# Sparse attention and a rational feed-forward layer: residue-split scores, batched normalisation, a chunk pipeline and a computed order of instructions

## The chip, the cores and the metric

The kernel runs on 1 core of one Trainium2 chip. The metric is device time in microseconds (us). Engines are named as the profile does: PE (TensorE, with PEld for its weight loads), DVE (VectorE), ACT (ScalarE), POOL (GpSimd), SP (SyncE, which here only issues transfers). A "q" behind an engine's name in a profile line ("SPq") means the engine's sequencer issuing a transfer.

## The reference

```
q, k, v: [8 batches, 8 heads, 576 tokens, 64], f32
scores = q @ k^T / 8
heads 0..3: keep 0 <= i-j < 32                      (local)
heads 4..7: keep j <= i and i % 32 == j % 32        (strided)
attn = softmax(scores);  o = attn @ v
x = o as [4608, 512];  h = x @ w_in                 (512 x 2048)
P = a0 + a1 h + a2 h^2 + a3 h^3
Q = 1 + |b0| |h| + |b1| h^2
out = (P / (Q + 1e-6)) @ w_out                      (2048 x 512, f32 out)
```

## The kernel before

The kernel takes 9 chunks of 512 tokens one after another: attention of one batch, first product, rational function, second product. Three parts matter here. Attention treats each head and each key tile by itself: scores into one bank, a mask added by a matmul with the identity, an exponential on ACT, a matmul with the values (with a column of ones, so that the row sums come along), then a reciprocal and a multiplication per head.

```python
ev_rc = emit(QDVE, Sdve, lambda d, ...: d.reciprocal(
    rcol[rl][r0:r0 + ns, 0:1], acc[r0:r0 + ns, VST * j + 64:VST * j + 65]), ...)
ev_nm = emit(QDVE, Sdve, lambda d, ...: d.tensor_scalar(
    XR[xslot][r0:r0 + ns, h * D:(h + 1) * D], acc[r0:r0 + ns, VST * j:VST * j + 64],
    rcol[rl][r0:r0 + ns, 0:1], None, op0=Alu.mult), ...)
```

The dense part has one set of buffers, and the output tile is copied by DVE:

```python
for f in range(NF):                     # 16 tiles of the first product, two banks
    psh = ps_h[f % 2]
    ... 4 matmuls (Win x XT) ...
    ACT: hbT[:, f, :] = copy(psh)
... rational function on hbT in pieces of 128 x 2048, one z and one u buffer ...
for m in range(TPC):                    # second product, one bank
    ... 16 matmuls (LG x Wout) ...
    DVE: outsb = copy(ps_out)
    POOL: store outsb
```

The casts from f32 to bf16 are issued by POOL, batch by batch, two heads at a time; the order in which instructions stand on each engine is written by hand.

The softmax here doesn't subtract the row's maximum and nothing guards it: scores larger than these inputs give would overflow.

## Time and profile before

| | before |
|---|---|
| median (range) | 924.05 us (923.52 to 924.86), 3 runs |
| busy, share of the span | PE 64%, DVE 50%, ACT 37% |
| mean granted clock (see the caution under "Reading the second hundred") | 0.724 |
| period per chunk, read from the timeline | about 99 us |

These lines are from the page of the kernel before. First the busy times; then rows of 40 slices of 23.1 us each, one digit a slice (busy share in tenths, for PEclk the granted clock in tenths); then the chain of waits that ended last, as shares of the span; then groups of instructions (count, busy us, mean ns of one, idle time before them and what ended it).

```profile
PE 593.8 (64%) x2704; PEld 255.2 (28%) x2704; DVE 460.7 (50%) x1001; ACT 345.3 (37%) x569; POOL 154.4 (17%) x167
...
PE   0493496469744985499628974698549854915706
...
DVE  0131059522954098416941495319540984393681
ACT  0131155406460437124531555053704371261540
...
PEclk9999975589556955596559755795569555967959
...
PE 53%; DVE 23%; ACT 15%; SPq 3%; DMA 2%; issue 2%; POOL 2%; DVEq 0%; POOLq 0%
...
L626 PE MATMUL ps_out<-Wout,lgt 128*128 128x512 bf16 x576 | 148.2, 416 | 152.0 <-DVE lgt L594 130.8
...
L516 ACT ACTIVATE hbt<-ps_h 128x512 bf16<-128x512 f32 x144 | 86.0, 597 | 309.4 <-PE ps_h L507 309.4
L435 DVE RECIPROCAL rcol<-ps_acc 128x1 f32<-128x1 f32 (+1 forms) x320 | 51.1, 160 | 268.5 <-PE ps_acc L407 266.8
...
L443 DVE TENSOR_SCALAR X<-ps_acc,rcol 128x64 bf16<-128x64 f32 (+1 forms) x320 | 90.8, 284 | 11.4
...
L304 POOL DMA_DIRECT2D ks<-in_k_dram x32 | 80.5, 4383 | 4.0 <-issue 4.0
```

No engine is full. The digits of PE and DVE go up and down in turn: the stages stand one behind the other, and the chain is handed from PE to DVE to ACT. The clock row sits at 5 to 7 for most of each period. Normalising costs DVE 51.1 + 90.8 = 142 us, in 640 small instructions.

### The profile page before, as it was taken

What the parts mean: (1) busy time and instruction counts of PE and PEld (TensorE: products, weight loads), DVE (VectorE), ACT (ScalarE), POOL (GpSimd) and SP (SyncE); (2) the same over time, 40 slices, a digit from 0 to 9 for tenths busy, and PEclk for the clock granted to TensorE, in tenths of its full rate; (3) what the DMA queues carried; (4) which work ended last, traced back from release to release, by engine and by line L of the source; (5) the groups of instructions that cost most, each with busy time, mean ns of one, the idle gap of its engine ahead of it and who ended that gap; (6) DMA issues with size and microseconds to landing.
All of it is one profiled execution on the core that took longest, in us unless ns stands there. A gap on an engine that the chain in (4) does not pass through costs nothing.

```text
span 924.9 us, 7533 instructions
## 1 busy us (share of the span) xinstructions
PE 593.8 (64%) x2704; PEld 255.2 (28%) x2704; DVE 460.7 (50%) x1001; ACT 345.3 (37%) x569; POOL 154.4 (17%) x167
## 2 busy tenths in 40 slices
PE   0493496469744985499628974698549854915706
PEld 0241142224321342134213432244213421302202
DVE  0131059522954098416941495319540984393681
ACT  0131155406460437124531555053704371261540
POOL 9986000240006000600020000000000000000000
PEclk9999975589556955596559755795569555967959
DMA  9999901490109010931051010101010000100001
GB/s 120 137 156 192 99 19 20 36 116 25 26 8 128 24 26 13 94 71 26 14 49 59 13 26 16 50 24 25 0 46 23 1 1 18 57 0 23 23 0 45
DMA packets 180868, 42.73 MB, mean 46 GB/s; under 512 B 175712, under 2 KB 178016, under 8 KB 180832
## 3 DMA queue, kind: packets, MB, share of 16 engines
q0 software_dynamic: 118016, 27.80, 30.7%
q1 hardware_dynamic: 62816, 14.47, 9.4%
q8 instruction: 21, 0.34, 0.2%
q14 instruction: 15, 0.12, 0.0%
HBM read 36.98 MB, written 18.87 MB: 60 GB/s over the span
## 4 chain that ended last, share of the span: by engine, by line
PE 53%; DVE 23%; ACT 15%; SPq 3%; DMA 2%; issue 2%; POOL 2%; DVEq 0%; POOLq 0%
PE ps_out L626 16%; PE ps_h L507 14%; PE ps_score L371 8%; PE ps_score L384 8%; PE ps_acc L407 7%; ACT lgt L573 7%; ACT qmt L581 5%; DVE lgt L594 5%; DVE chz L589 3%; DVE X L443 3%; ACT ET L391 3%; DVE outsb L636 2%; SPq L481 2%; DVE qmt L543 1%; DVE chu L554 1%
## 5 line engine op out<-in xcount | busy, mean ns | idle before, releaser
L626 PE MATMUL ps_out<-Wout,lgt 128*128 128x512 bf16 x576 | 148.2, 416 | 152.0 <-DVE lgt L594 130.8
L391 ACT ACTIVATE ET<-ps_score 128x192 bf16<-128x192 f32 (+5 forms) x352 | 126.6, 369 | 225.0 <-PE ps_score L384 195.5
L516 ACT ACTIVATE hbt<-ps_h 128x512 bf16<-128x512 f32 x144 | 86.0, 597 | 309.4 <-PE ps_h L507 309.4
L435 DVE RECIPROCAL rcol<-ps_acc 128x1 f32<-128x1 f32 (+1 forms) x320 | 51.1, 160 | 268.5 <-PE ps_acc L407 266.8
L407 PE MATMUL ps_acc<-vb,ET 128*128 128x65 bf16 (+3 forms) x784 | 127.0, 244 | 79.0 <-ACT ET L391 76.2
L371 PE MATMUL ps_score<-qT,kT 64*128 64x192 bf16 (+5 forms) x352 | 129.2, 367 | 28.7 <-DMA kT<-ks 28.7
L626 PEld LDWEIGHTS ps_out<-Wout,lgt 128*128 128x128 bf16 x576 | 57.8, 106 | 239.9 <-DVE lgt L594 132.7
L407 PEld LDWEIGHTS ps_acc<-vb,ET 128*128 128x128 bf16 (+3 forms) x784 | 75.7, 118 | 136.1 <-ACT ET L391 99.0
L636 DVE COPY outsb<-ps_out 128x512 f32<-128x512 f32 x36 | 24.9, 692 | 151.6 <-PE ps_out L626 151.6
L645 POOL DMA_DIRECT2D out_dram<-outsb x36 | 19.7, 548 | 468.3 <-DVE outsb L636 468.3
L443 DVE TENSOR_SCALAR X<-ps_acc,rcol 128x64 bf16<-128x64 f32 (+1 forms) x320 | 90.8, 284 | 11.4
L289 POOL DMA_DIRECT2D vb<-in_v_dram x40 | 36.3, 939 | 289.2 <-PE ps_acc L407 289.2
L304 POOL DMA_DIRECT2D ks<-in_k_dram x32 | 80.5, 4383 | 4.0 <-issue 4.0
L384 PE MATMUL ps_score<-MS,IDN 128*128 128x512 bf16 (+2 forms) x192 | 78.1, 407 | 0.9
L304 POOL DMA_DIRECT2D qs<-in_q_dram x32 | 77.0, 3952 | 3.4 <-issue 3.4
L573 ACT ACTIVATE lgt<-qmt,consts 128x2048 bf16<-128x2048 bf16 x36 | 69.4, 1990 | 15.9 <-DVE qmt L543 15.9
L507 PE MATMUL ps_h<-XT_0,Win 128*128 128x512 bf16 x144 | 55.3, 384 | 28.9 <-DMA XT_3<-X 28.9
L581 ACT ACTIVATE qmt<-lgt 128x2048 bf16<-128x2048 bf16 x36 | 65.6, 1896 | 0.0
L507 PE MATMUL ps_h<-XT_1,Win 128*128 128x512 bf16 x144 | 55.3, 384 | 0.0
L507 PE MATMUL ps_h<-XT_2,Win 128*128 128x512 bf16 x144 | 55.3, 384 | 0.0
L507 PE MATMUL ps_h<-XT_3,Win 128*128 128x512 bf16 x144 | 55.3, 384 | 0.0
L371 PEld LDWEIGHTS ps_score<-qT,kT 64*128 64x128 bf16 (+1 forms) x352 | 36.5, 104 | 65.6 <-DMA kT<-ks 28.8
(27 smaller groups left out, 496.6 us busy)
## 6 DMA issues: line engine op xcount, KB each, us to landing
out_dram<-outsb POOLq DMA_DIRECT2D x36, 256.0 KB, 2.3
qs<-in_q_dram POOLq DMA_DIRECT2D x32, 144.0 KB, 9.2
ks<-in_k_dram POOLq DMA_DIRECT2D x32, 144.0 KB, 9.5
vb<-in_v_dram POOLq DMA_DIRECT2D x32, 128.0 KB, 4.7
Win<-in_moe_w_in_dram POOLq DMA_DIRECT2D x4, 512.0 KB, 16.5
Wout<-in_moe_w_out_dram POOLq DMA_DIRECT2D x16, 128.0 KB, 22.0
XT_0<-X SPq DMA_TRANSPOSE x36, 3.1
XT_1<-X SPq DMA_TRANSPOSE x36, 2.4
```

The costliest lines, as they stand in the source:

```text
L304: lambda p, b=b, pair=pair, src_t=src_t, dst_t=dst_t: p.dma_start(dst_t[b, pair, :, :].rearrange("s (hh d) -> s hh d", hh=2), src_t[b, 2 * ...
L371: e.matmul(ps[0:nk, 0:x1 - x0], kT[tslot][pbase:pbase + 64, tk0:tk0 + nk], qT[tslot][pbase:pbase + 64, x0:x1], start=True, stop=False),
L384: e.matmul(ps[0:nk, 0:W], IDN[0:nk, 0:nk], mrhs, start=False, stop=True),
L391: a.activation(ET[esl][0:nk, 0:W], ps[0:nk, 0:W], AF.Exp, scale=0.125),
L407: return e.matmul(acc[rb:rb + M, VST * j:VST * j + 65], ET[esl][0:nk, ov0 - x0:ov0 - x0 + M], vb[slot][0:nk, ktile, h, 0:65], start=False, ...
L435: d.reciprocal(rcol[rl][r0:r0 + ns, 0:1], acc[r0:r0 + ns, VST * j + 64:VST * j + 65]),
L443: d.tensor_scalar(XR[xslot][r0:r0 + ns, h * D:(h + 1) * D], acc[r0:r0 + ns, VST * j:VST * j + 64], rcol[rl][r0:r0 + ns, 0:1], None, op0=Al ...
L507: e.matmul(psh[:, 0:CH], Win[kk][:, f * 128:(f + 1) * 128], XT[cs][kk][:, 0:CH], start=(kk == 0), stop=(kk == NK1 - 1)),
L516: a.activation(hbT[:, f, :], psh[:, 0:CH], AF.Copy),
L573: lambda a, qmT=qmT, lgT=lgT, f0=f0: a.activation(lgT[:, f0:f0 + G, :], qmT[:, f0:f0 + G, :], AF.Ln, bias=eps1_ap, scale=1.0),
L581: lambda a, qmT=qmT, lgT=lgT, f0=f0: a.activation(qmT[:, f0:f0 + G, :], lgT[:, f0:f0 + G, :], AF.Exp, scale=-1.0),
L626: e.matmul(pso[:, 0:Fout], LG[0][:, kk, m * 128:(m + 1) * 128], Wout[kk][:, 0:Fout], start=(kk == 0), stop=(kk == NK2 - 1)),
```

## The change

Its intent: compute the strided heads as dense small problems (tokens are split by their residue modulo 4, so that the mask wastes less), join exponentials into wide calls, normalise a whole tile of 128 tokens and 8 heads with two DVE instructions, double the buffers of the dense part, move the output copies to ACT, and let a list scheduler (an estimate of each instruction's cost, a priority key, and the rule "the free engine takes the ready instruction with the smallest key") compute the order in which the instructions stand on each engine. The diff rewrites nearly the whole kernel; its core:

```diff
-  NQT = 6; qT, kT [128, NKT*128] per head pair      # one bank, 352 score calls
-  ev_rc = reciprocal(... one head ...)               # x320
-  ev_nm = tensor_scalar(... one head ...)            # x320
+  o2 = add("DVE", lambda d: d.reciprocal(rc[:, :, :], psA[:, :, 64:65]), ..., 0.25, key - 20)
+  o3 = add("DVE", lambda d: d.tensor_tensor(x.rearrange("x (h d) -> x h d", h=8),
+           psA[:, :, 0:64], rc.to_broadcast([128, 8, 64]), op=Alu.mult), ..., 0.75, key - 20)
-  z, u, hbT, qmT, lgT, t3T: one buffer each, pieces of 128 x 2048
+  NHB = 2; NT3 = 2; NU = 2; NGB = 4                  # pieces of 128 x 4096
-  DVE tensor_copy(outsb, ps_out)
+  ACT activation(OS, psO, Copy)
-  casts issued per batch and head pair, by hand-written order
+  for b in range(B):                                 # all 24 casts, with no dependence at all
+      for nm, s_, d_ in (("q", q, qc), ("k", k, kc), ("v", v, vc)):
+          add("POOL", lambda e: e.dma_start(d_[b]..., s_[b]...), [], 1.2, key, g, 5.0)
+  ... relayouts ql<-qc, kl<-kc and transposes, all on SP, each with an assumed cost of 0.1 us ...
+  add("SP", fn, [cast[nm, b].ops], 0.1, key, grel, 3.0)
+  pr.schedule()                                      # list scheduler: order for each engine
   ... (cut)
```

The names in the new kernel: `qc`, `kc`, `vc` are the bf16 copies in device memory, `ql`, `kl` a second layout of them, `qS`, `kS`, `qL`, `kL` the transposed tiles for strided and local heads; `psS` holds scores, `psA` attention outputs, `XR` the normalised tile, `XT` its transpose, `psH` and `psO` the two products, `ZZ`, `UU`, `T`, `GB` the rational function.

## The prediction

> **What bounds it now.** Nothing is saturated: the page gives PE 64% of the span, DVE 50%, ACT 37%, and the chain of waits is handed around (PE 53%, DVE 23%, ACT 15%). The kernel runs its stages one after another. The timeline shows a period of about 99 us per chunk: some 65 us of attention mixed with the rational chain, then 14.4 us of second product (16 matmuls in 3.64 us, four times, evacuations of 0.70 us between them) and 13.8 us of first product (64 matmuls, 216 ns apart), during which DVE and ACT nearly stand still (ACT waits 309 us for the first product's banks). The granted clock alternates: 0.5 for about 65 us, 1.0 for about 34 us. [...]attention, with its small waits, runs at 0.5 throughout.
>
> **Work after the change (all estimates from trace durations).**
> - DVE. Rational chain in 8x512 pieces: the 2048-wide operations take 0.69 to 0.81 us (scalar, uncontended) and 1.23 us (two tensors); doubled width adds about 0.53 and 1.07, so about 15.7 us a group, 18 groups, 282 us (was about 302, with contention). Normalising: 40 x (0.17 + about 0.7) = 35 us instead of 51 + 91 = 142. The 25 us of output copies go to ACT. Sum about 325 us with gaps, instead of 461. POOL now issues about 150 small output transfers; where POOL issued transfers, a scalar operation took 1.35 instead of 0.75 us, so I add 30 us: about 355.
> - ACT. First-product copies 86, Ln/Exp 135, output copies 22, exponentials 45 (was 127: about 40,000 columns in 48 wide calls): about 290 us.
> - PE. Products 1152 x 0.22 = 253 us at full clock. Attention per batch: 80 score matmuls, 132 value matmuls, many of odd shapes. In the trace a 256-column matmul that alternates between 64 and 128 rows takes 0.21 to 0.22 us at full clock, about twice its streaming time. [...]The new order still alternates shapes, so I take 18 to 24 us a batch, 150 to 190 in all. Sum 400 to 440 us at full clock.
> - SP queue: about 25 plain issues (0.43), 8 transposes (1.25) and 5 X transposes (1.25 to 4) a batch, 27 to 41 us: close, not the limit.
>
> **Critical path.** Start: casts, relayout and transposes until about 30 us; batch 0 alone, score rounds bouncing PE to ACT through one buffer, until about 65 to 70. Then stages overlap, PE slightly ahead of DVE as the limit, 43 to 50 us per chunk instead of 99; a tail of about 20 us (second product of the last chunk). 68 + about 385 + 20, plus some 3% of ordering losses, is about 485 us. Range 425 to 560. Chances: faster 0.97, same 0.02, slower 0.01.
>
> **What would show it.** DVE busy 320 to 370 us and at 70 to 80% of the span; ACT 280 to 300; granted clock near 1.0 from about 80 us on; no 28 us stretches where ACT and DVE stand still; first rational operation at 65 to 80 us; the chain mostly PE and DVE; X normalise near 0.7 us x40.
>
> **What would make it wrong.** PE staying at half clock (work then doubles: 600 us and more); the in-order SP queue holding X transposes behind waiting loads; POOL issues slowing DVE more than assumed; static orders made from wrong costs, engines then waiting for each other; or shape switches cheaper than assumed and loads earlier (430 or less).

Where a cut is marked, words went that held no term of the sum. That is still 68 + about 385 + 20, and about 12 of ordering losses: 485 us. The 18 to 24 us a batch for attention on PE is the author's estimate; "twice its streaming time" is against 108 ns, half of the 216 ns at which the 512-column matmuls of before follow each other (an estimate). The 0.53 and 1.07 us for doubled width were estimates too: measured in after it is 0.54 (0.68 to 1.22 us, the fastest scalar operation) and 1.05 (1.23 to 2.28 us, two tensors).

## The result

| | before | after |
|---|---|---|
| median (range) | 923.78 us (922.62 to 924.86), 4 runs | 597.87 us (597.27 to 599.32), 4 runs |
| ratio after/before | | 0.6476, 95% interval 0.6465 to 0.6486 |
| mean granted clock | 0.724 | 0.934 |
| busy: PE, DVE, ACT | 594, 461, 345 us | 390, 303, 272 us |

The column "before" has one run more than the table above. A ratio here is the mean time of one kernel's fast runs over the mean of the other's fast runs of the same rounds, so it is not quite the ratio of the medians that stand beside it.

The direction was right and the size was not: 485 us was predicted, with 425 to 560 as the range. These are the lines of the page after that answer to those of before (a slice is now 14.9 us):

```profile
PE 390.4 (66%) x2801; PEld 185.2 (31%) x2848; DVE 303.3 (51%) x259; ACT 272.3 (46%) x301; POOL 114.6 (19%) x196
...
PE   0000000233349259899999999999999999998572
...
DVE  1000000000011049988869668768868986999910
ACT  0000000120104009976756757757756757988510
...
PEclk9999999999999559999979979979979979999987
...
PE 46%; SPq 30%; DVE 10%; issue 4%; ACT 4%; POOL 3%; DMA 2%; DVEq 0%; POOLq 0%
...
L520 PE MATMUL psO<-Wout,GB 128*128 128x512 bf16 x551 | 147.3, 396 | 18.1 <-ACT OS L784 9.3
...
L716 ACT ACTIVATE HB<-psH 128x512 bf16<-128x512 f32 x144 | 82.5, 600 | 63.7 <-PE psH L520 62.6
...
L650 DVE RECIPROCAL RC<-psA 128x8 f32<-128x8 f32 x40 | 8.2, 205 | 180.0 <-PE psA L520 180.0
...
L652 DVE TENSOR_TENSOR XR<-psA,RC 128x512 bf16<-128x512 f32 x40 | 27.4, 686 | 30.5 <-DMA XT<-XR 30.2
```

Read the rows of digits first. From the sixteenth slice on, PE is nearly a row of nines, and DVE and ACT work at the same time: the overlap that the change was made for is there. Normalising fell from 142 to 8.2 + 27.4 = 36 us, the second product no longer waits (152 us of idle time before it became 18). But PE's first seven slices, over 100 us, are zeros, and the next eight are thin but for one. The chain has a new member: 30% of the span is SP issuing transfers.

The windows view, cut at three events of the trace (first score matmul 113.5 us, first operation of the rational function 213.9, end of its last operation 567.3), gives the same in numbers. Its columns are the stretch, its length, the busy us of PE, PEld, DVE, ACT and POOL with their instruction counts, the granted clock, the DMA share and GB/s.

```profile
0.00:45.00 45.00, 0.00 (x0) 0.00 (x0) 2.18 (x17) 1.28 (x1) 17.29 (x36) 1.00 0.99 201
...
113.50:213.90 100.40, 44.54 (x452) 20.68 (x458) 7.98 (x18) 18.27 (x24) 0.00 (x0) 0.91 0.59 99
213.90:567.30 353.40, 331.42 (x2294) 159.04 (x2334) 293.11 (x225) 250.32 (x272) 82.05 (x128) 0.93 0.31 60
567.30:595.40 28.10, 14.43 (x55) 5.50 (x56) 0.02 (x1) 2.39 (x4) 15.25 (x32) 0.80 0.17 38
```

So the time is 214 us of start, 353 of middle and 28 of tail. The prediction had 68, 385 and 20, and 12 of ordering losses. The start alone is 146 us over; the middle is 32 us better than predicted. In the middle PE is busy for 331 of 353 us: there the new order works. The question is what the first 214 us are.

**Reading the start.** The list of waits (total us, times, longest us) puts 113.5 us to one event, the transposed local keys:

```profile
PE psS L520 <- DMA kL<-kl: 128.8, 2, 113.5
```

The timeline of SP (start, duration, engine, source line, operation, count) shows what came before it. These are of batch 0, but for the last line, which is the first of batch 1:

```profile
7.51 40.92 SPq L461 DMA_DIRECT2D ql<-qc  x4
48.48 11.91 SPq L472 DMA_TRANSPOSE qS<-qc  x2
60.44 33.73 SPq L465 DMA_DIRECT2D kl<-kc  x4
...
110.67 1.27 SPq L478 DMA_TRANSPOSE kL<-kl  x1
111.98 2.67 SPq L461 DMA_DIRECT2D ql<-qc  x4
```

Four small relayouts kept SP for 40.9 us. The same four of the next batch took 2.67 us. Meanwhile the DMA share is 0.99: POOL had issued all 24 casts and all 8 weight loads between 1.3 and 18.3 us. They are 24 x 576 KB + 8 x 512 KB, about 18.4 MB; at the 201 GB/s of the window above that is 91 us (an estimate), and the DMA row of the page stays at 0.9 until about 90 us. The four relayouts stood behind that heap (e1_paced below, without it, has them at 6.15 us).

**Reading the second hundred.** Between the first scores and the first rational operation lie another 100 us, in which PE works 44.5. The first normalised tile was ready early; its line in the DVE timeline is

```profile
128.95 0.69 DVE L652 TENSOR_TENSOR XR<-psA,RC 128x512 bf16<-128x512 f32 x1
```

and its transpose, which the first product needs, was issued by SP only here:

```profile
161.11 1.26 SPq L667 DMA_TRANSPOSE XT<-XR  x1
```

It is 31 us later, behind relayouts and transposes of the next batches. SP takes its instructions in a fixed order, and the scheduler computed that order with 0.1 us for each issue. The timeline has 0.43 to 0.68 us for a plain one and 1.19 to 1.31 for a transpose, 128x512 and 576x128 alike. A batch's transfers from SP land 1.9 to 3.0 us after their issue (medians by kind, from the DMA view), but the issues stand one behind the other. Added up for a batch from the quiet parts of the timeline (8 relayouts 5.3, 8 transposes 10.3, 17 value loads 9.8, 5 transposes of `XR` 6.5) that is 32 us of issuing; the scheduler believed 38 x 0.1 = 3.8 us, thought SP nearly free, and so saw no harm in placing other batches' loads first.

One caution on the clock figures. The first record of the clock in this trace begins at 182 us, and the views count the time before it as 1.00. The matmuls say otherwise; these are eight of the first product just before and eight just after that moment:

```profile
178.62 3.59 PE L520 MATMUL psH<-XT,Win 128*128 128x512 bf16 x8 [6.48 <-DMA XT<-XR]
...
182.96 1.90 PE L520 MATMUL psH<-XT,Win 128*128 128x512 bf16 x8
```

The first of them start 427 ns apart, as they do where the record has 0.5, and the later ones 216 ns apart, as where it has 1.0. So TensorE's first work ran at half clock, and the means (0.91 for this stretch, 0.934 and, for the same reason, the 0.724 of before, whose record begins at 111 us) are somewhat too high.

**Reading the middle.** The clock row of the page falls to 7 in about every third slice of the middle. The fifth token tile of each batch (64 tokens) is where it happens. The PE timeline, with start and duration (ends are modelled, so neighbours overlap):

```profile
297.64 0.81 PE L520 MATMUL psO<-Wout,GB 128*128 128x512 bf16 x3 [0.16 <-issue]
...
302.89 0.20 PE L520 MATMUL psA<-vs,ES 128*16 128x65 bf16 x1
303.02 0.19 PE L520 MATMUL psA<-w,ES 16*16 16x65 bf16 x1
303.14 0.20 PE L520 MATMUL psA<-vs,ES 128*16 128x65 bf16 x1
...
307.11 0.22 PE L520 MATMUL psA<-w,ES 16*16 16x65 bf16 x1
307.66 1.49 PE L520 MATMUL psO<-Wout,GB 128*128 128x512 bf16 x3 [0.34 <-issue]
```

Shapes alternate, 125 to 150 ns apart, for 40 matmuls in 5.5 us (from 301.84 us on). About 3 us into it, where the pitch goes from 125 to 150 ns, the granted clock drops to 0.5, and it stays there for 6.8 us by the clock's records, so that after the tile three ordinary matmuls take 1.49 us instead of the 0.81 of the first line. Seven fifth tiles lie in the middle. Six are followed by such a dip, five of 6.8 us and one of 3.4; the other, the earliest, lies in a stretch of half clock that had begun before it.

### The profile page after: what moved, and what is told of

The parts are those of the page before. It is cut to its first block, busy times and chain, and to the rows that moved or that the text cites. A ratio compares the mean times of both kernels' runs of the same rounds, so it can differ in the third digit from the quotient of the medians.

```text
span 595.4 us, 6854 instructions
## 1 busy us (share of the span) xinstructions
PE 390.4 (66%) x2801; PEld 185.2 (31%) x2848; DVE 303.3 (51%) x259; ACT 272.3 (46%) x301; POOL 114.6 (19%) x196
## 4 chain that ended last, share of the span: by engine, by line
PE 46%; SPq 30%; DVE 10%; issue 4%; ACT 4%; POOL 3%; DMA 2%; DVEq 0%; POOLq 0%
PE psH L520 16%; PE psO L520 15%; PE psA L520 10%; SPq L461 9%; SPq L465 8%; SPq L472 5%; PE psS L520 4%; SPq L478 3%; POOL out_dram L799 3%; DVE GB L756 2%; DVE T L751 2%; DVE T L747 2%; ACT UU L737 1%; SPq L495 1%; DMA qc<-in_q_dram 1%
## 5 line engine op out<-in xcount | busy, mean ns | idle before, releaser
L791 POOL DMA_DIRECT2D out_dram<-OS x128 | 82.1, 647 | 462.5 <-ACT OS L784 462.1
L520 PE MATMUL psO<-Wout,GB 128*128 128x512 bf16 x551 | 147.3, 396 | 18.1 <-ACT OS L784 9.3
L520 PE MATMUL psH<-XT,Win 128*128 128x512 bf16 x558 | 146.9, 399 | 12.6 <-DMA XT<-XR 6.5
L716 ACT ACTIVATE HB<-psH 128x512 bf16<-128x512 f32 x144 | 82.5, 600 | 63.7 <-PE psH L520 62.6
L520 PEld LDWEIGHTS psO<-Wout,GB 128*128 128x128 bf16 x576 | 54.8, 101 | 88.0 <-ACT OS L784 16.0
L520 PEld LDWEIGHTS psH<-XT,Win 128*128 128x128 bf16 x576 | 56.0, 102 | 81.0 <-issue 11.8
L737 ACT ACTIVATE UU<-UU,cst 128x2048 bf16<-128x2048 bf16 x36 | 71.7, 2001 | 4.2 <-DVE UU L730 4.2
L740 ACT ACTIVATE UU<-UU 128x2048 bf16<-128x2048 bf16 x36 | 68.8, 1911 | 0.1
L756 DVE TENSOR_TENSOR GB<-T,UU 128x4096 bf16<-128x4096 bf16 x18 | 41.1, 2284 | 4.1 <-ACT UU L740 3.9
L652 DVE TENSOR_TENSOR XR<-psA,RC 128x512 bf16<-128x512 f32 x40 | 27.4, 686 | 30.5 <-DMA XT<-XR 30.2
L751 DVE TENSOR_TENSOR T<-T,HB 128x4096 bf16<-128x4096 bf16 x18 | 41.1, 2283 | 0.3
L747 DVE TENSOR_TENSOR T<-T,HB 128x4096 bf16<-128x4096 bf16 x18 | 40.9, 2273 | 0.1
L730 DVE TENSOR_TENSOR UU<-UU,ZZ 128x4096 bf16<-128x4096 bf16 x18 | 40.9, 2271 | 0.0
```

What stands on the lines that cost most here:

```text
L520: return lambda e: e.matmul(out_ap, l, r, start=start, stop=stop, skip_group_check=True)
L716: o2 = add("ACT", (lambda a, hb=hb, hi=hi, fi=fi: a.activation(hb[:, fi, :], psH[hi][:, :], AF.Copy)), [o1, hb_free[ig % NHB]], 0.6, key - 30)
L730: d3 = add("DVE", (lambda d, u=u: d.tensor_tensor(u[:, :, :], u[:, :, :], ZZ[:, :, :], op=Alu.mult)), [d2], ctt, key + 0.02)
L737: ln = add("ACT", (lambda a, u=u, sl=sl: a.activation(u[:, sl, :], u[:, sl, :], AF.Ln, bias=cst[:, 0:1], scale=1.0)), [d3, cons], 0.28 + H ...
L740: ex = add("ACT", (lambda a, u=u, sl=sl: a.activation(u[:, sl, :], u[:, sl, :], AF.Exp, scale=-1.0)), [ln], 0.28 + HG * CH * 0.000833, key ...
L747: d5 = add("DVE", (lambda d, hb=hb, t3=t3: d.tensor_tensor(t3[:, :, :], t3[:, :, :], hb[:, :, :], op=Alu.mult)), [d4], ctt, key + 0.04)
```

## The experiments

Theory: the start is long for two reasons, casts that fill the DMA engines before the first small transfers (A), and an SP order made from wrong costs (C); the sparse fifth tile and its half clock (D) lengthen the middle. The rivals: the start is work that no order can hide (transfers and scores of one batch take that long by themselves); the middle is what PE and DVE need anyway; and for A, that it is the size of the casts' packets that delays others, not their number. First and last rows are the kernels before and after. "First score" and "first rational" are times in the profiled run; "middle" ends with the last operation of the rational function.

| run | median us | ratio to before, 95% | first score | first rational | middle | tail |
|---|---|---|---|---|---|---|
| after | 597.87 | 0.6465 to 0.6486 | 113.5 | 213.9 | 353.4 | 28.1 |
| e1_paced | 561.62 | 0.6018 to 0.6098 | 37.9 | 137.7 | 387.5 | 33.5 |
| e2_spcost | 564.56 | 0.6098 to 0.6121 | 114.9 | 165.9 | 369.5 | 28.1 |
| e2b_spcost | 555.69 | 0.5974 to 0.6035 | 104.7 | 165.6 | 359.9 | 28.7 |
| e3_both | 533.27 | 0.5736 to 0.5786 | 38.6 | 116.9 | 374.9 | 35.4 |
| e4_t4 | 557.79 | 0.6022 to 0.6064 | 113.4 | 213.1 | 313.8 | 29.5 |
| e4b_t4 | 559.47 | 0.601 to 0.6079 | 113.4 | 213.6 | 316.0 | 29.3 |
| f1_small | 595.31 | 0.6419 to 0.6454 | 109.0 | 209.5 | 356.6 | 28.1 |
| b2_all | 518.33 | 0.5567 to 0.5644 | 45.1 | 92.4 | 388.4 | 35.2 |
| b5 | 486.58 | 0.5155 to 0.5244 | 41.0 | 89.4 | 366.1 | 32.0 |
| b7 | 522.34 | 0.56 to 0.5671 | 46.2 | 93.2 | 388.8 | 34.9 |
| b8 | 503.08 | 0.5405 to 0.5484 | 49.5 | 115.3 | 346.7 | 34.4 |
| b10 | 500.99 | 0.5402 to 0.543 | 49.8 | 113.3 | 355.1 | 30.6 |
| e5_order | 900.0 | 0.9676 to 0.9774 | 104.4 | 195.2 | 662.6 | 40.3 |
| e6_single | 670.44 | 0.7223 to 0.7262 | 113.3 | 213.6 | 430.2 | 29.5 |
| e8_pernorm | 730.75 | 0.7884 to 0.7926 | 113.3 | 210.7 | 489.5 | 27.5 |
| before | 924 | 1 | | | | |

All runs were correct by the comparison with the reference (but see e4_t4). Medians are of four runs each (five for e6_single). Two of b5's four runs, its profiled one among them, and one each of e1_paced and b8 were over 1.5% above the fastest of the same kernel and count as slow; the ratios use the fast ones only, and b5's stages are those of a slow run (489.24 us).

### e1_paced: casts held back

The casts of batch b+1 (and the weights) wait until the loads of batch b have landed. As in most of the experiments, the scheduler then computes all orders anew.

```diff
+    held.setdefault(b, []).extend(g.ops)         # at each cast (batch 0's are never held)
+    held.setdefault(1, []).extend(g1.ops)        # first weights with batch 1
+    held.setdefault(2, []).extend(g2.ops)        # second weights with batch 2
+    for o in held.get(b + 1, []):                # at the end of loads(b)
+        o.deps.extend(tr_ev[b] + v_ev[b])
```

> The casts and weight loads of a later batch wait until the loads of the batch before have landed; nothing else changes. Theory A (all 24 casts and 8 weight loads, queued in the first 18 us, fill the DMA engines for 95 us and starve batch 0's small relayout transfers): first matmul at 25 to 40 us instead of 113.5, first rational operation at 110 to 140 instead of 214, total 500 to 540. Rival B (the relayout chain of small transfers and transposes is itself slow, whatever else moves): first matmul stays above 90 us and the total within 2% of 598.

Measured: 561.62 us, 36 us less than after. The first score came at 37.9 us instead of 113.5. The SP timeline of this run, to be held beside that of after:

```profile
7.20 6.15 SPq L466 DMA_DIRECT2D ql<-qc  x4
13.40 2.61 SPq L477 DMA_TRANSPOSE qS<-qc  x2
16.06 2.60 SPq L470 DMA_DIRECT2D kl<-kc  x4
```

The same issues of 40.9, 11.9 and 33.7 us take 6.2, 2.6 and 2.6. So A is shown: the wait of the first 113 us was the heap of casts, not the loads of batch 0. But of 76 us gained at the first score only 36 arrive at the end. The total misses the 500 to 540 that were expected. The middle grew from 353 to 388; my reading, not tested apart here, is that the casts are still to be moved, now beside the loads of the next batches.

### f1_small: is it the packets' size?

In the trace of after the casts' packets are of 18432 bytes and took 1391 ns in the mean. If it is the size of these packets that holds up the small transfers, smaller packets should free the start without any pacing. The casts were cut into pieces of 1024 elements over 16 rows instead of pieces that merge to 9216:

```diff
-   d_[b].rearrange("h s d -> (h s d)").rearrange("(r c) -> r c", c=2048)
+   d_[b].rearrange("h s d -> (h s d)").rearrange("(p r c) -> r p c", r=16, c=1024)
    (the source likewise)
```

> Only the shape of the 24 casts changes: the same bytes, in pieces of 1024 elements (2 KB written) instead of 9216 (18 KB, 1.39 us a packet in the trace of the kernel after). Nothing is held back, nothing reordered. Theory A2 ([...]it is the size of the cast packets that starves them): the four ql transfers take 5 to 15 us to issue instead of 41, first matmul at 45 to 75 us instead of 113.5, total 540 to 575. Rival (the bytes queued in front decide, whatever their pieces): first matmul above 100 us, total within 2% of 598.

Measured: 595.31 us, within 0.6% of after. The SP timeline:

```profile
7.42 15.82 SPq L461 DMA_DIRECT2D ql<-qc  x4
...
40.42 14.08 SPq L465 DMA_DIRECT2D kl<-kc  x4
```

Single groups of issues did get faster, 40.9 to 15.8 us and 33.7 to 14.1. But other issues of the chain became slower in exchange (`qS` 17.1 instead of 11.9 us, `vt` x4 17.2 instead of 2.2), and the first score came at 109 us instead of 113.5. The whole row of batch 0's transfers still crawled until the casts were through (the DMA share was 1.21 from 60 to 90 us; from 96.8 us on an issue of `vo` took 0.43 us again). The rival with the packets falls as an explanation of the time, as far as this step goes: the same bytes in front, in packets of 2048 bytes and 171 ns, cost the same start. Those packets are still 8 to 16 times the relayouts' own (128 and 256 bytes); smaller ones were not tried.

### e2_spcost and e2b_spcost: true issue costs for the scheduler

Nothing that runs is changed, only the costs with which the order is computed.

```diff
-   add("SP", fn, [cast[nm, b].ops], 0.1, key, grel, 3.0)
+   add("SP", fn, [cast[nm, b].ops], 0.66, key, grel, 3.0)
-       [cast[nm, b].ops, fr], 0.1, key + 0.1, gt, 3.0)
+       [cast[nm, b].ops, fr], 1.30, key + 0.1, gt, 3.0)
    ... qL, kL: 1.27; value loads: 0.57; XT<-XR: 1.31 ...
```

> Only the scheduler's cost of one issue on the SP queue is changed, from 0.1 us to what the trace shows (0.43 to 0.66 plain, 1.27 to 1.31 transposes), so only static orders change. Theory C (the SP queue's order, made from wrong costs, puts relayouts of later batches in front of the X transposes): first matmul stays at about 113 us, but the first rational operation moves from 214 to 150 to 175 us and the total falls to 545 to 570. If order is not the matter: total within 2% of 598.

> As e2_spcost (SP issue costs as in the trace), but without a slip of that edit, which had also moved the priority of the qS and kS transposes behind the loads of v. Theory C: first matmul still near 113 us, first rational operation at 150 to 170, total 545 to 570, as in e2_spcost, whose slip should cost or gain less than 8 us.

e2_spcost had a slip: the replacement also turned `key + 0.1` into `key + 1.30`, so the transposes of `qS` and `kS` moved behind the value loads in priority. e2b_spcost mends it. Measured: 564.56 and 555.69 us. In e2b_spcost the first score is still late (104.7 us), as the casts are not held, but from there to the first rational operation it takes 61 us instead of 100. Its SP timeline has the transposes of `XR` in groups, before the next batch's relayout is finished:

```profile
140.89 4.44 SPq L667 DMA_TRANSPOSE XT<-XR  x3
```

So C is shown: with the same instructions and better costs the kernel is 42 us faster. e3_both repeats the slip.

### e3_both: pacing and costs together

```diff
    (the edits of e1_paced and of e2_spcost, slip included)
```

> Both edits. If A and C hold and act on different stretches, the gains add: first matmul at 25 to 40, first rational operation at 65 to 85, total 455 to 490, which is where the prediction was. If one hides the other, the total is that of the better single edit.

Measured: 533.27 us. Against after that is 65 us less; the two alone gave 36 and 33 (with the slip, as here), so they add up nearly in full, 70. The 455 to 490 that were expected are missed all the same, and the middle is 375 us, longer than after's 353.

### e4_t4 and e4b_t4: the fifth tile's matmuls grouped by shape

The 16 small ones are issued after the 16 larger ones instead of in turn with them.

```diff
+   late = []
-   makers.append(mm(o, ES[...], vs[iv][:, h, g, 0:65], True, False))
+   makers.append(mm(o, ES[...], vs[iv][:, h, g, 0:65], h == 0, False))
-   makers.append(mm(o, ES[32*g:...], w4[iv][32*g:...], False, True))
+   late.append(mm(o, ES[32*g:...], w4[iv][32*g:...], False, True))
+   makers.extend(late)
```

> In the fifth token tile of each batch the 16 value matmuls of 128 rows x 16 columns and the 16 of 16 rows x 16 columns no longer alternate: all of the first shape, then all of the second. Theory D (each change of shape costs about 0.1 us more than the streaming, and the sparse stretch halves the granted clock for 6.8 us afterwards): the 40-matmul group falls from 5.3 to about 2 us, the half-clock stretches after it vanish, and the total falls by 30 to 50 us (PE is the limit between 250 and 490 us). Rival: the pitch of about 130 ns is what small matmuls cost in any order; the group stays above 4.5 us and the total within 2%.

> As e4_t4 with the same matmuls in the same order, but only the first matmul of each PSUM bank and quadrant carries the start flag[...]. Values are now those of the kernel after. Time: as e4_t4, 553 to 562 us, since no matmul is added or removed.

e4_t4 kept the start flag `True` in every large matmul. In a simulation of the program's values (on no chip) that went wrong: for tokens 512 and up of a batch the result had a relative error of 5.4% (root mean square), while all other kernels gave the values of the kernel before, bit for bit. The chip's comparison with the reference passed it, so no run here shows the error on the chip, nor what the flag does there. e4b_t4 sets the flag for the first head only, and its simulated values are right. Its time, 559.47 us, is within 0.3% of e4_t4's. These are its lines for the fifth tile:

```profile
295.88 0.30 PE L520 MATMUL psA<-vs,ES 128*16 128x65 bf16 x16
296.11 0.30 PE L520 MATMUL psA<-w,ES 16*16 16x65 bf16 x16
296.57 0.81 PE L520 MATMUL psO<-Wout,GB 128*128 128x512 bf16 x3 [0.16 <-ACT UU L742]
```

32 matmuls that took 4.4 us take 0.5, and the matmuls behind them run at full clock. In the windows view cut by the same events (columns as above) the middle has changed from a clock of 0.93 and 331 us of PE to this:

```profile
213.60:529.60 316.00, 296.84 (x2294) 140.59 (x2334) 292.58 (x225) 249.33 (x272) 90.36 (x128) 0.98 0.35 67
```

D is shown, and it is worth 38 us for a few moved lines: PE's busy time in the middle fell by 35 us. Most of it is the tiles' own pitch: seven tiles in the middle at 3.9 us each are some 27 us (an estimate), which leaves about 11 us for the half clock behind them. The rival ("the middle is what PE needs anyway") falls.

The traces show what a change of shape costs: 125 to 150 ns a matmul where shapes alternate (after) and about 15 ns where they do not (e4b_t4: 16 in 0.23 us, the change to the other shape included). In e4b_t4's trace the sixteen start in fours, 3 to 4 ns apart within a four and 18 to 25 ns from one four to the next, and the first matmul of the other shape starts 121 ns after the last of them; in the trace of after the sixteen of 128x32 at 278.82 us have 1 to 5, 21 to 29 and 124 ns. So a change of shape costs about 0.12 us here, and in the alternating order no four start together. As for the clock, the timeline of after shows PE as busy all along the 5.5 us, and the clock fell about 3 us into them. If the 65 columns of such a matmul stream in 27 ns (an estimate from 512 columns in 216 ns), columns stream for about a fifth of a pitch of 133 ns. Grouping removed the pitch and the half clock together; which property of the stretch brings the clock down is not shown. The shorter alternating stretches of the other tiles (8 matmuls, 1.06 us) are not followed by half clock: the record of after is at 1.0 past the one at 284.04 us, until 304.95 us.

### b2_all: the three together

Pacing (as e1_paced, but each batch's casts one batch earlier, and batch 1's held until batch 0's relayout), true costs, the grouped fifth tile with the local heads of the other tiles grouped too, priority for the transposes of `XR`, and half of the last outputs on SP.

```diff
    (e2b_spcost, e4b_t4, and)
+   if b == 0: for o in held[1]: o.deps.extend(grel.ops)
+   for o in held.get(b + 2, []): o.deps.extend(tr_ev[b] + v_ev[b])
-   [o3, wait], 1.31, key - 20, gx, 3.0)
+   [o3, wait], 1.31, key - 60, gx, 3.0)
-   add("POOL", ... last chunk's outputs ...)
+   add("SP" if m % 2 else "POOL", ...)
    ... (cut)
```

> Everything together: casts of batch 1 and the first weights wait for batch 0's relayouts, later casts for the loads of two batches before; SP costs as measured and X transposes given priority; the value matmuls of a token tile grouped by shape; half of the last chunk's output transfers on the SP queue. If the three causes (starved start, order on SP, sparse shape-alternating matmuls) are the whole miss: first matmul at 26 to 34 us, first rational operation at 75 to 95, no half-clock stretches in the middle, about 35 us a chunk with DVE as the limit, total 420 to 455 us. If another cause remains, above 480.

Measured: 518.33 us. The first rational operation is at 92 us, so the start is repaired for the most part. But the middle is 388 us, although with the fifth tile alone it was 316: a miss. SP is now 37% of the chain. The last outputs on SP brought nothing: the tail is 35 us.

### b5: value loads on POOL

To take 17 of a batch's issues from SP, the value loads are issued by POOL, and the casts are of the small pieces of f1_small.

```diff
-   add("SP", lambda e: e.dma_start(vt[i][...], vc[b, ...]), base, 0.57, key, gv, 3.0)
+   add("POOL", lambda e: e.dma_start(vt[i][...], vc[b, ...]), base, 0.85, key, gv, 3.0)
    (and the other four value loads)
```

> b2_all with two further edits: cast pieces of 1024 elements, and the 17 loads of v per batch issued by POOL instead of SP. Theory E (in b2_all the SP queue is what is left: about 31 us of issues a batch, stretched to 45 by casts in flight): SP per batch falls to 22 to 26 us, first rational operation at 70 to 90, total 440 to 475. If SP is not the limit of b2_all: total within 2% of 518.

Measured: 486.58 us (477.32 to 494.64; fast runs 477.32 and 483.91). It beats both kernels and is the fastest of all that were run: 0.5199 of the time of before. The 440 to 475 us that were expected are missed. SP is down to 10% of the chain; the price is POOL, busy 208 us instead of 112. The gain belongs to the value loads: b7 below, with the same pieces, without the hold on batch 1's casts and with the value loads on SP, ran in 522 us, as b2_all did.

### b7, b8 and b10: why the middle stayed long

Open was whether the early batches wait for loads or the middle overlaps badly by itself. b7 is b2_all with the small pieces and without the hold on batch 1's casts and the first weights; b8 has in addition the value loads of batches 0 to 2 on ACT's queue; b10 those of batches 0 and 1 only.

```diff
    (b7)
-   if b == 0: for o in held[1]: o.deps.extend(grel.ops)
    (b8; b10 with b < 2)
-   add("SP", ... value loads ...)
+   add("ACT" if b < 3 else "SP", ... value loads ...)
```

> b2_all's repairs, the casts of 1024-element pieces, and the casts of batch 1 and the first weight no longer held back behind batch 0's relayout; the v loads stay on the SP queue. Theory (the early batches wait for data: casts arrive late because they are held, SP issues about 45 us a batch at first): first rational operation 85 to 100 us, middle 345 to 375, total 470 to 515; SP stays the pacing queue of batches 1 and 2. Rival (the middle of 366 to 388 us of b2_all and b5 is PE and DVE work that overlaps badly, whatever the loads do): the middle stays above 380 and the total at 500 to 525.

> As b7, but the v loads of batches 0 to 2 are issued from the ACT queue, which has little to do then, so that SP issues only the q, k relayouts and transposes early: about 13 us of issue a batch less on SP. Theory (SP issue and late loads set the early pace): first rational operation 75 to 90 us, middle 325 to 355, total 430 to 475, below b7 by 25 us or more. Rival (work that overlaps badly, or the casts' traffic itself): within 10 us of b7, with DVE waiting in 90 to 165 us as in b5.

> As b8, but only the v loads of batches 0 and 1 are issued from the ACT queue; those of batch 2, which in b8 stood at 86 to 105 us in ACT's order in front of the first copies of the first product (first such copy 107 us, first rational operation 115 us against 93 in b7), go back to SP. Theory (in b8 the in-order ACT queue held the start back, and SP's relief shortened the middle): first rational operation 80 to 98 us, middle 345 to 370, total 465 to 495. Rival (v loads elsewhere only move the same wait): total within 8 us of b8's 503, first rational operation still above 108 us.

b7 measured 522.34 us, the same as b2_all, with a middle of 389: these are the figures of its rival, and the hold on batch 1's casts was not the reason. Its SP timeline shows how two of the relayouts of batches 1 and 2 went:

```profile
59.80 7.17 SPq L470 DMA_DIRECT2D kl<-kc  x2
...
101.56 10.14 SPq L470 DMA_DIRECT2D kl<-kc  x2
```

The same pair takes 1.30 us where no casts are in flight. With such stretches a batch's loads keep SP from 54.5 to 97.1 us, 43 us instead of about 32, which is as long as a whole batch takes PE. In b7's windows of 50 us between 100 and 300 us PE is busy only for 19 to 42 us while the DMA share is 0.79 to 0.91; in the two windows from 350 to 450 us, where the casts are through, PE is busy for over 48.

b8 measured 503.08 us, 19 less than b7, less than the theory asked for. Its middle did fall, from 389 to 347 us, as the theory said; but its first rational operation came 22 us later. My explanation for that was ACT's order: the value loads of batch 2 stand there before the first copies of the first product. b10 took just these away, and the first rational operation stayed at 113.3 us, the total at 500.99: that explanation fell. The SP timeline of b10 shows what the two have in common:

```profile
77.81 9.06 SPq L678 DMA_TRANSPOSE XT<-XR  x1
...
90.72 6.13 SPq L678 DMA_TRANSPOSE XT<-XR  x1
```

With fewer issues on SP the scheduler places batch 2's relayouts between the transposes of batch 0's tiles, and their issue then takes 9.06 and 6.13 us instead of 1.26: POOL had issued three casts and four weight loads between 74.5 and 79.2 us, and the DMA engines were full then (the DMA row of b10's page has 9 in both slices from 75 to 100 us), so the transfers in front were probably held up by these. So the early batches do wait for loads (b8's middle shows it), but lightening SP without thinning the casts only moves the wait. The way from here to the sum of the single gains stays open; no version was found that has an early start and a short middle together.

### e5_order: the change without the scheduler's order

Each engine takes its instructions in the order in which the program creates them.

```diff
+   order = {e: [o for o in self.ops if o.eng == e] for e in self.ENGS}    # replaces the computed order
    self.order = order
```

> The kernel after with the list scheduler's orders replaced by the order in which the program creates its operations (batch's loads, scores, values, first product, second product). If the scheduler's orders carry the overlap: 68 to 80 us per chunk instead of 44, total 700 to 850. If the shorter instruction streams and double buffers carry it: total within 6% of 598.

Measured: 900.0 us, only 2.7% less than before. One window of 100 us in the middle of it (columns as above; in after the same window has PE at 97.67 us, clock 0.90):

```profile
300.00:400.00 100.00, 63.59 (x367) 27.37 (x372) 39.52 (x31) 34.07 (x37) 11.83 (x24) 0.70 0.25 47
```

All the savings in work are in this run, fewer and larger instructions, double buffers, and they bring 2.7%. The order brings the rest, 900 to 598 (700 to 850 were expected of this run). The order of creation is one plain order; a careful order by hand was not tried. That does not make the other parts worthless, as the next two runs show.

### e6_single and e8_pernorm: two parts undone under the scheduler

```diff
    (e6_single)
-   NHB = 2; NT3 = 2; NU = 2
+   NHB = 1; NT3 = 1; NU = 1
    (e8_pernorm)
-   one reciprocal and one tensor_tensor for 8 heads
+   for h in range(8): reciprocal(rc[:, h, :]); tensor_scalar(xv[:, h, :], psA[:, h, 0:64], rc[:, h, :])
```

> The kernel after with one buffer instead of two for the first product's output, the polynomial and the denominator (HB, T3, UU), orders scheduled anew. If the double buffers carry part of the overlap: 48 to 56 us per chunk instead of 44, total 625 to 700. If they do not matter: within 2% of 598.

> The kernel after with the normalisation per head again: 8 reciprocals and 8 multiplications a token tile instead of one of each, orders scheduled anew. DVE gains about 40 x (8 x 0.44 - 0.89) = 105 us of work, and becomes the limit of the middle (about 47 us a chunk instead of 44): total 615 to 680. If DVE had slack enough everywhere: within 2% of 598.

Measured: 670.44 us and 730.75 us. So the double buffers are worth 73 us and batched normalising 133, once the order is there to use them. Normalising by head costs DVE what it cost before:

```profile
L655 DVE TENSOR_SCALAR XR<-psA,RC 128x64 bf16<-128x64 f32 x320 | 90.4, 283 | 12.3 <-DMA XT<-XR 3.3
...
L653 DVE RECIPROCAL RC<-psA 128x1 f32<-128x1 f32 x320 | 53.4, 167 | 240.1 <-PE psA L520 232.1
```

That is 143.8 us against 35.6, 108 more, and the time grows by 133, above the 615 to 680 us that were expected. Two things in the trace go with it. The computed order places operations of the rational function between the 16 small ones of a tile, so that a tile's normalising takes 4.1 us at best and 16 to 28 us for 12 of the 40 tiles (2.0 in the median of after), in which the single buffer `psA` stays taken. And within the middle the second product now waits 71 us for the rational function on DVE, for which it did not wait in after. How the two share the 133 us is not shown, and an order that keeps a tile's operations together was not tried.

## Why the prediction was right or wrong

- **"Faster" with 0.97: right.** The ratio is 0.648.
- **"Start: casts, relayout and transposes until about 30 us": this is the step that failed.** It took batch 0's chain by itself. In a quiet queue the chain does take about 30 us (e1_paced: 7.2 to 36.4 us). In the kernel as it is, 18.4 MB of casts and weights without any dependence stand in front, and the first score came at 113.5 us. The numbers were there to be read: the diff gives the casts an empty list of dependences, and 18.4 MB at the 192 GB/s that the page of before shows in its best slice is 96 us (an estimate). In the kernel before, whose casts are smaller, ordered batch by batch and keep POOL for 4.4 us each, the first score came at 35.9 us.
- **"Batch 0 alone ... until about 65 to 70": failed as well.** From the first score to the first rational operation 100 us passed, not 35 to 40. The prediction knew that SP was "close, not the limit", at 27 to 41 us a batch (measured about 32 when quiet, 43 with casts in flight), and it named "the in-order SP queue holding X transposes behind waiting loads" and "static orders made from wrong costs" among the things that would make it wrong. Both came true; they should have stood in the sum. The source has the scheduler's 0.1 us beside a trace of before with about 1.25 us a transpose.
- **"43 to 50 us per chunk": the middle was right and a little too long.** It is 353 us; the fifth tiles in it follow each other by 39 to 48 us. "PE slightly ahead of DVE as the limit" is right: 331 of 353 us busy. The prediction's 400 to 440 us for PE was 390 at a clock of 0.93; with the fifth tile grouped it is 353 (e4b_t4). "The new order still alternates shapes" was the right thought, and the 150 to 190 us in the sum for the attention matmuls more than cover what they took (130, and 99 in e4b_t4). What was not in the sum is the half clock that such a stretch leaves to the matmuls behind it, about 11 of the 38 us that grouping gains.
- **DVE: 355 us predicted, 303 measured.** The term that was too large is "I add 30 us" for POOL's issues slowing DVE. In before two scalar operations (at 282.28 and 285.00 us) took 1.35 and 1.33 us while POOL issued casts, against 0.74 for the same one at 277.62 us before these; in after the scalar operations of double width take 1.22 to 1.34 us, as estimated without any slowing. That is 30 of the 52 us; the groups themselves sum to 280 and 36 us, as predicted (282 and 35), and the busy time of the engine counts their overlaps once. POOL's issues grew instead, from 0.55 to 0.65 us each. Share of the span 51%, not 70 to 80%, because the span is longer at its start.
- **ACT 280 to 300 us: 272. XR near 0.7 us x40: 0.686 x40. Clock near 1.0 from 80 us on: 0.93 as the views count it, with half clock until 182 us and the dips of the fifth tile. The chain "mostly PE and DVE": PE 46%, but then SP 30%.** (The prediction's "0.5 throughout" for attention in before is nearly so: of the batch that begins at 222 us, the first 5 us ran at 1.0.)
- **The tail of 20 us: 28.** Besides the second product of the last chunk, the last 32 output issues keep POOL for 15.25 us, as the timeline shows, and they begin only after the first output tile is there:

```profile
574.71 15.25 POOL L799 DMA_DIRECT2D out_dram<-OS  x32 [11.80 <-issue]
```

The sum of the miss: +146 for the start, -32 for the middle, +8 for the tail, -12 for the "3% of ordering losses" that was spread over the rest, which is +110 of the 113 us; the profiled span is 2.5 us shorter than the median time. With the faults of the start and the fifth tile repaired, b5 runs in 487 us, about the predicted figure; that is a different kernel, and not a confirmation.

## What to carry to other kernels

Transfers without dependences are not free work to be issued first (18.4 MB of them put the first score at 113.5 us here, 37.9 when paced): add up their bytes, divide by the rate in the trace, and ask which small transfer stands behind them. A computed order is only as good as its costs (42 us in e2b_spcost), so put measured ones in for the issuing queue too. And a stretch of small matmuls of alternating shapes such as the 5.5 us here costs twice, in its own pitch (4.4 us for 32 matmuls, 0.5 when grouped) and in the clock of what follows (0.5 for 6.8 us); grouping them by shape was a cheap cure here, 38 us, with the start flags set as in e4b_t4.
